# A fused attention and gated feed-forward kernel: each engine's instructions given as a fixed sequence from the kernel's own list schedule

## The chip, the cores and the metric

The kernel runs on one core of one Trainium2 chip. The metric is the device time of one execution in microseconds; lower is better. Before the change three runs gave 1300.32, 1300.39 and 1302.6 us, median 1300.39.

## The reference

Attention with queries pooled in pairs, then a gated feed-forward block whose gate mixes along the sequence. Batch 8, 8 heads, 1152 keys, 576 pooled queries, head size 64; model width 512, inner width 1024.

```python
q_pool = q.reshape(B, H, S // 2, 2, D).mean(axis=3)
scores = matmul(q_pool, k.transpose(0, 1, 3, 2)) / sqrt(D)
attn = exp(scores - scores.max(-1)); attn = attn / (attn.sum(-1) + 1e-09)
x = matmul(attn, v).transpose(0, 2, 1, 3).reshape(B, S // 2, H * D)
h = maximum(x @ w_in, 0); u, g = h[..., :512], h[..., 512:]
g_n = (g - g.mean(-1)) / sqrt(g.var(-1) + 1e-06)
g_s = einsum('ts,bsd->btd', w_spatial, g_n) + b_spatial[None, :, None]
out = (u * g_s) @ w_out
```

## The kernel before

Work is staged by *head pairs*, two heads of one batch: 32 of them, numbered i. Every matrix is split into a large and a small half-precision part, so a product of two matrices is two or three matmuls.

For a head pair `prep` scales queries and keys, splits them, and lays the parts out by DMA in `qhi`, `khi`, `klo`, `xq` and `qd` (ACT L138, L141, L311, L313; DVE L144; POOL L298, L314; a dozen DMAs, L305 to L323). `maxima` makes the scores once coarsely, 27 matmuls of 384 columns (L341, L350), each reduced on DVE (L356). The maxima are then transposed on PE (L371) and enter the precise scores as two more rows. `attention` makes these in 18 steps of 512 queries (L524, L525) and some tail pieces; ACT takes the exponential (L530, L538), and POOL subtracts the rounded part from what it was rounded from (`split`, L542, on 128x1024). `values` multiplies by the values (L444, L448, L453: twelve matmuls of 64 or 65 columns a step), four steps or more later. `turn_main` transposes the result (L475) and writes it as `xg` (ACT L417, DVE L418).

The two weights arrive as doubles. `from_double` decodes a piece of 128x512 in five DVE instructions (L155, L158, L160, L164, L166) and two on ACT; there are twelve pieces. A *unit* is the feed-forward block of two batches: `gated_unit` runs after the eight head pairs that feed it (L601, L665, L706, L749 on PE; the norm L637, L643 on DVE), in the background of the next eight. The last of the four units runs after all attention.

The program is traced by Python generators which are advanced in turn: maxima of i+1, values ahead, prep of i+2, weights and the unit are each moved a little at every step of the attention of i. What is traced is not the final order. The framework's scheduler orders the instructions of each engine by its own estimates, and each engine then runs its list strictly from the front: the first instruction that is not ready holds all behind it. SP issues all DMAs from one such list.

PSUM tiles come from pools: `ps_s` three (pss), `ps_m` two (pm), `ps_w` two (pw), `ps_o` one (o). A third pm tile can be written only when the last reader of the first one is done. So a *slot* joins PE to DVE and ACT: PE stands until a reduction, or the copy of `xg`, has emptied it.

Of the kernel before, what the change touches and what calls it, by code (L numbers as in the profile page):

```python
# [10 lines left out]
F16 = mybir.dt.float16  # L11
BF16 = mybir.dt.bfloat16
F32 = mybir.dt.float32
I32 = mybir.dt.int32
I64 = mybir.dt.int64
U32 = mybir.dt.uint32
# [3 lines left out]
PSUM = bass.MemoryType.PSUM  # L20
# [8 lines left out]
PEXP = 2.0 ** 6  # L29


@with_exitstack
def attn_sgu_kernel(ctx: ExitStack, tc: tile.TileContext, qT, kT, v, w_in, w_spT, b_sp, w_out, out):
    nc = tc.nc
    P = 128
    B, NHP, _, D, _, S = qT.shape
# [18 lines left out]
    D1 = D + 1  # L55
    VW = 2 * D + 2

    const = ctx.enter_context(tc.tile_pool(name="const", bufs=1))
    ld = ctx.enter_context(tc.tile_pool(name="ld", bufs=1))
    pp = ctx.enter_context(tc.tile_pool(name="pp", bufs=4))  # L60
    pt_ = ctx.enter_context(tc.tile_pool(name="pt_", bufs=1))
    wk = ctx.enter_context(tc.tile_pool(name="wk", bufs=2))
    mo = ctx.enter_context(tc.tile_pool(name="mo", bufs=1))
    sm = ctx.enter_context(tc.tile_pool(name="sm", bufs=1))
    ps_s = ctx.enter_context(tc.tile_pool(name="ps_s", bufs=3, space=PSUM))
    ps_m = ctx.enter_context(tc.tile_pool(name="ps_m", bufs=2, space=PSUM))
    ps_o = ctx.enter_context(tc.tile_pool(name="ps_o", bufs=1, space=PSUM))
    ps_w = ctx.enter_context(tc.tile_pool(name="ps_w", bufs=2, space=PSUM))


    nc.scalar.preload_act_table_set("natural_log_exp_and_others")
# [203 lines left out]
    def values_ahead(i):  # L275
        if i + NHP < NP:
            yield from norm_v(i + NHP)
        if i + 1 < NP:
            yield from split_v(i + 1)
# [47 lines left out]
    def maxima(i):  # L327
        st = state[i]
        qhl, khh, X = st["qhl"], st["khh"], st["X"]
        W = KEYS // 3  # L330
        NB = W // P
        mt = sm.tile([P, NT, 3], F32, name="mt", bufs=2)
        for t in range(NT):
            for n in range(3):

                if units or (t + n) % 2:
                    pm = ps_m.tile([P, 512], F32, name="pm")
                else:
                    pm = ps_w.tile([P, 512], F32, name="pw")
                if t == 4:  # L340
                    nc.tensor.matmul(  # L341
                        pm[:, :W],
                        lhsT=qd[i % 2].rearrange("p h s -> p (h s)"),
                        rhs=st["kn"][:, n * NB : (n + 1) * NB, :],
                        start=True, stop=True,
                    )
                else:
                    h = 0 if t < 4 else 1
                    c0 = t * P if t < 4 else TAIL + (t - 5) * P
                    nc.tensor.matmul(  # L350
                        pm[:, :W],
                        lhsT=qhl[:, h, c0 : c0 + P],
                        rhs=khh[:, h, n * NB : (n + 1) * NB, :],
                        start=True, stop=True,
                    )
                nc.vector.reduce_max(out=mt[:, t, n : n + 1], in_=pm[:, :W], axis=AX.X)  # L356
                yield

            if t == 4 and True:
                yield from shift(X, mt, 0, 5)  # L360
        yield
        yield from shift(X, mt, 5 if True else 0, NT)
# [40 lines left out]
    xs = {}  # L403
# [392 lines left out]
    def step(gen):  # L796
        return None if gen is None or next(gen, StopIteration) is StopIteration else gen
# [13 lines left out]
    def drain(gen):  # L811
        while gen is not None:
            gen = step(gen)
# [13 lines left out]
    for i in range(NP):  # L827
        if i + 2 < NP:
            load_kq(i + 2)
        run = [  # L830
            Pace(maxima(i + 1), MAX_RATE) if i + 1 < NP else None,
            Pace(values_ahead(i), V_RATE),
            Pace(prep(i + 2), PREP_RATE, PREP_AT) if i + 2 < NP else None,
            Pace(weights, W_RATE, W_AT if i == 0 else 0),
        ]
# [17 lines left out]
        turn(last=True)  # L853
    for g in units:
        drain(g)


def _lay(inputs):
# [42 lines left out]
```

## Time and profile before

| what | us |
|---|---|
| median of three runs | 1300.39 |
| the profiled execution, whole | 1304.26 |
| its span, first to last instruction | 1302.1 |
| PE busy, of the span | 1179.4 |
| ACT busy | 978.1 |
| DVE busy | 903.9 |
| POOL busy | 847.8 |

PE is TensorE's matmuls, DVE VectorE, ACT ScalarE, POOL GpSimd, SP the engine that issues DMAs. Three stages can be told apart by what runs in them. The first exponentials are at 38.9 us, and attention then runs without a unit until the first matmul of a unit at 302.8. From there on three units run beside attention until the last of the attention's work is near, about 1171. What remains is mostly the fourth unit. The whole execution is 2.2 us longer than its span.

### The profile page before, as it was taken

Reading aid. Unit: us, or ns where it says so; the run is one execution under the profiler, and the core shown is the slowest. Engines: PE = TensorE matmul, PEld = TensorE weight load, DVE = VectorE, ACT = ScalarE, POOL = GpSimd, SP = SyncE. Lnnn points to the kernel's source line nnn. Section 1 sums busy time; section 2 is a strip of 40 time slices with the busy share of each in tenths; the row PEclk is TensorE's granted clock in tenths of the full one; section 3 lists DMA queues with packets and bytes.
Section 4 is the critical chain, followed back from the end, with each engine's and each line's share of the span. In section 5 each row is a group of like instructions: output and inputs, shape, how many; then the busy total and the mean of one; then the engine's idle time right before and its main releaser. Section 6 shows DMA issues by size and latency. Waiting matters only on the chain.

```text
span 1302.1 us, 33821 instructions
## 1 busy us (share of the span) xinstructions
PE 1179.4 (91%) x13632; PEld 734.2 (56%) x13632; DVE 903.9 (69%) x2096; ACT 978.1 (75%) x1689; POOL 847.8 (65%) x494
## 2 busy tenths in 40 slices
PE   3888787789999999899998999899997999999998
PEld 1455554555555666566664666566654666555454
DVE  4689989986778567865669576865669756751545
ACT  5888888889977887878767877878775886755333
POOL 3798897888755766767675767767765666664000
PEclk9989999999999999999999999999998999999999
DMA  7555353435422333154233332155333211101002
GB/s 251 168 166 153 109 162 104 124 95 161 116 87 84 107 107 107 39 144 151 83 100 91 98 115 76 38 149 148 90 107 88 66 52 45 32 34 42 1 1 73
DMA packets 64029, 129.04 MB, mean 99 GB/s; under 512 B 13888, under 2 KB 22080, under 8 KB 63872
## 3 DMA queue, kind: packets, MB, share of 16 engines
q1 hardware_dynamic: 63872, 126.88, 33.7%
q8 instruction: 107, 1.75, 0.6%
q14 instruction: 50, 0.41, 0.1%
HBM read 83.56 MB, written 9.44 MB: 71 GB/s over the span
## 4 chain that ended last, share of the span: by engine, by line
PE 57%; DVE 21%; ACT 9%; POOL 6%; issue 4%; DMA 3%; POOLq 0%; SPq 0%; ACTq 0%; DVEq 0%
DVE mt L356 7%; PE pm L350 6%; PE pss L525 6%; PE pss L524 6%; PE pw L706 6%; PE pw L601 5%; PE pw L749 4%; POOL pt L542 4%; PE pw L665 3%; PE o L453 3%; PE o L444 3%; ACT pt L530 3%; PE o L448 3%; DVE vv L144 2%; DVE row L637 2%
## 5 line engine op out<-in xcount | busy, mean ns | idle before, releaser
L542 POOL TENSOR_TENSOR pt<-pt 128x1024 f16<-128x1024 f32 x288 | 565.6, 1969 | 226.6 <-ACT pt L530 221.4
L530 ACT ACTIVATE pt<-pss,lnp,esc 128x512 f32<-128x512 f32 x576 | 441.8, 779 | 145.5 <-PE pss L525 134.9
L356 DVE TENSOR_REDUCE mt<-pm 128x1 f32<-128x384 f32 x730 | 392.2, 552 | 142.0 <-PE pm L350 125.8
L525 PE MATMUL pss<-xq,klo 66*128 66x64 f16 (+1 forms) x1152 | 279.1, 292 | 0.0
L524 PE MATMUL pss<-qhi,khi 128*128 128x64 f16 (+1 forms) x1152 | 273.5, 291 | 3.2 <-ACT ptl L538 1.7
L350 PE MATMUL pm<-khi,qhi 128*128 128x384 f16 x652 | 213.0, 331 | 26.1 <-DVE mt L356 22.1
L444 PE MATMUL o<-vp,pt 128*128 128x65 f16 x2304 | 229.9, 195 | 6.2 <-DVE xm L461 6.1
L448 PE MATMUL o<-vp,pt 128*128 128x64 f16 x2304 | 228.8, 194 | 0.0
L444 PEld LDWEIGHTS <-pt 128*128 128x128 bf16 x2304 | 183.3, 99 | 71.8 <-DVE xm L461 11.0
L448 PEld LDWEIGHTS <-pt 128*128 128x128 bf16 x2304 | 169.2, 99 | 59.2 <-issue 15.8
L453 PE MATMUL o<-vp,pt 128*128 128x65 f16 x2304 | 170.2, 195 | 19.5 <-POOL pt L542 18.8
L453 PEld LDWEIGHTS <-pt 128*128 128x128 f16 x2304 | 113.0, 99 | 29.8 <-POOL pt L542 25.6
L525 PEld LDWEIGHTS <-klo 66*128 66x128 f16 x1152 | 98.2, 99 | 39.9 <-issue 11.2
L524 PEld LDWEIGHTS <-khi 128*128 128x128 f16 x1152 | 102.4, 100 | 28.4 <-issue 12.9
L272 POOL TENSOR_TENSOR vp<-vt,vp 128x576 f16<-128x576 f32 x64 | 82.6, 1291 | 45.1 <-ACT vp L270 45.0
L350 PEld LDWEIGHTS <-qhi 128*128 128x128 f16 x768 | 75.8, 100 | 63.2 <-issue 12.9
L542 POOL TENSOR_TENSOR ptl<-ptl 128x1152 f16<-128x1152 f32 x32 | 70.4, 2199 | 56.5 <-ACT ptl L538 56.4
L314 POOL TENSOR_TENSOR klo<-kt,kn 128x640 f16<-128x640 f32 x64 | 88.3, 1385 | 11.5 <-ACT kn L313 11.3
L538 ACT ACTIVATE ptl<-pss,lnp,esc 128x256 f32<-128x256 f32 (+1 forms) x128 | 75.5, 590 | 18.2 <-PE pss L525 18.1
L601 PE MATMUL pw<-wi_h,xg 128*128 128x512 f16 x240 | 89.1, 378 | 0.0
L356 DVE TENSOR_REDUCE mt<-pw 128x1 f32<-128x384 f32 x134 | 71.5, 544 | 17.0 <-PE pw L350 16.1
L665 PE MATMUL pw<-xg,wi_h 128*128 128x512 f16 (+1 forms) x336 | 82.0, 331 | 0.0
(180 smaller groups left out, 2356.8 us busy)
## 6 DMA issues: line engine op xcount, KB each, us to landing
vt<-in_v_dram SPq DMA_DIRECT2D x64, 576.0 KB
qt<-in_qT_dram SPq DMA_DIRECT2D x32, 576.0 KB
kt<-in_kT_dram SPq DMA_DIRECT2D x32, 576.0 KB
khi<-kn SPq DMA_DIRECT2D x128, 144.0 KB
out_dram<-row SPq DMA_DIRECT2D x24, 256.0 KB
qhi<-xq SPq DMA_DIRECT2D x64, 72.0 KB
klo<-klo SPq DMA_DIRECT2D x32, 144.0 KB
vv<-in_w_in_dram SPq DMA_DIRECT2D x8, 512.0 KB
```

The lines of the kernel that those rows point to most:

```text
L314: nc.gpsimd.tensor_sub(KL[:, 0, a:z], k0[:, a:z], kn[:, a:z])
L350: nc.tensor.matmul(pm[:, :W], lhsT=qhl[:, h, c0 : c0 + P], rhs=khh[:, h, n * NB : (n + 1) * NB, :], start=True, stop=True,)
L356: nc.vector.reduce_max(out=mt[:, t, n : n + 1], in_=pm[:, :W], axis=AX.X)
L444: nc.tensor.matmul(o[:, t], lhsT=top[:, cols], rhs=vp[:, D : D + D1], start=c == 0 and t == 0, stop=False, skip_group_check=True,)
L448: nc.tensor.matmul(o[:, t, 0:D], lhsT=top[:, cols], rhs=vp[:, 0:D], start=False, stop=False, skip_group_check=True)
L453: nc.tensor.matmul(o[:, t], lhsT=rst[:, cols], rhs=vp[:, D : D + D1], start=False, stop=c == NC - 1, skip_group_check=True,)
L524: nc.tensor.matmul(o, lhsT=khh[:, h, c, :], rhs=qhl[:, h, q], start=True, stop=False)
L525: nc.tensor.matmul(o, lhsT=KL[0:KR, h, c, :], rhs=X[0:KR, h, q], start=False, stop=True)
L530: nc.scalar.activation(pt, ps, AF.Exp, bias=lnp, scale=esc)
L542: nc.gpsimd.tensor_sub(t.bitcast(F16)[:, :, 0::2], t, t.bitcast(BF16)[:, :, 1::2])
L601: nc.tensor.matmul(ph, lhsT=xa[:, cc, c0 : c0 + P], rhs=wa[:, cc, DH:DF], start=n == 0, stop=n == 3 * NCC - 1,)
L665: nc.tensor.matmul(pu[:, : z - a], lhsT=wa[:, cc, fc * P : (fc + 1) * P], rhs=xa[:, cc, a:z], start=n == 0, stop=n == 3 * NCC - 1,)
```

## The change

The traced program is the same, instruction for instruction. New is a class `Order`. Its `pool` wraps every tile pool so that each tile's name, number and number of buffers are known. At the end of the kernel `pin` takes the traced instructions, finds which must wait for which (`edges`), gives each a duration from a small table (`cost`) and makes a list schedule: again and again it takes the engine whose next instruction can start soonest, and on it the earliest traced one that is ready by then. On DVE and POOL, instructions whose inputs all lie in SBUF exclude each other in the table's time. The order that comes out is handed to the framework as a chain of dependencies on each engine.

```diff
+    def edges(self, prog):
...
+                    used = users.setdefault(name, [])
+                    used.append(n)
+                    pre.add(used[0])
...
+    def cost(self, lane, ins):
...
+        if lane == "PE":
+            n = count(xs[0])
+            t = max(28.5, n / 2.4 + 2.5)
+            if xs[0].dtype == F32:
+                t = 110 if n == 128 else max(224, 4 * n / 2.4)
+            return t, t + 148
+        if lane == "SP":
+            big = max((count(x) * x.ap[0][1] * self.SIZE[x.dtype] for x in xs), default=0)
+            return 500, 2400 + big / 230
+        n = max((count(x) for x in xs), default=1)
+        psum = any(self.slot.get(x.tensor.name, (0, 0))[1] for x in xs)
+        if lane == "Activation":
+            t = 1.04 * n + (230 if psum else 95)
+        elif lane == "DVE":
+            t = 1.04 * n + 130
+        else:
+            t = (1.75 if any(x.dtype in (F16, BF16) for x in xs[:-1]) else 2.2) * n + 120
+        return t - 80, t
...
+    def pin(self, tc):
...
+        before = self.edges(prog)
...
+        for _ in prog:
+            best = None
+            for e, ns in ready.items():
+                if ns:
+                    t = max(free[e], min(due[n] for n in ns))
+                    n = min(n for n in ns if due[n] <= t)
+                    if best is None or t < best[0]:
+                        best = (t, e, n)
+            t, e, n = best
+            ready[e].remove(n)
+            own, out = cost[n]
+            if shared[n]:
+
+                if e == "DVE":
+                    if t >= held[0]:
+                        t = max(t, held[1] - 130)
+                    dve = t + out
+                else:
+                    t = max(t, dve)
+                    held = (t, t + out)
+            if e == "SP":
+                wire = max(wire, t + own) + (out - 2400)
+                end = wire + 1900
+            else:
+                end = t + out
+            free[e] = t + own
+            if e in last:
+                tc.add_manual_dep(prog[n], last[e], dep, reason="order")
+            last[e] = prog[n].name
...
-    const = ctx.enter_context(tc.tile_pool(name="const", bufs=1))
+    order = Order()
+    const = order.pool(ctx.enter_context(tc.tile_pool(name="const", bufs=1)), 1)
...
     for g in units:
         drain(g)
+    order.pin(tc)
```

What moved is read from the order of the built programs. The kernel's lines stand 195 lower in the changed file, so L316 is L511 there; a number behind a tile's name tells the tiles of one name apart.

**The start of the program.** The first maxima (L350) need both halves of `khi0`, two DMAs from `kn_163`. On SP, before, they stand four rows apart (L316, L317), ahead of the next bulk loads:

```order
L316 DMA khi0_116<-kn_163 64x1152
L305 DMA qhi0_119<-xq0_113 64x576
L306 DMA qhi0_119<-qhi0_119 64x576
L308 DMA qd0_122<-xq0_113 64x64 x2
L317 DMA khi0_116<-kn_163 64x1152
L318 DMA qhi0_119<-xq0_113 64x576
```

On SP now, from the first of the two (L511) to the second (L512):

```order
L511 DMA khi0_116<-kn_163 64x1152
L517 DMA klo0_107<-klo0_107 64x1152
L426 DMA kt_178<-in_kT_dram 128x1152
L425 DMA qt_346<-in_qT_dram 128x1152
L379 DMA vv_420<-in_w_in_dram 128x512
L432 DMA vt_186<-in_v_dram 128x2x576
L503 DMA qd0_122<-xq0_113 64x64
L513 DMA qhi0_119<-xq0_113 64x576
L512 DMA khi0_116<-kn_163 64x1152
```

Four bulk loads have moved in between: keys, queries, a piece of the weights and values. (`edges` lets every later user of a tile wait for the tile's first one; L512 is traced second on `khi0`, so in the schedule it waits for L511 to land.)

On DVE at the same place, before, one piece of the weights is decoded around the first reductions (`mt_203`):

```order
L155 TENSOR_SCALAR vv_420<-vv_420 128x512
L158 SCALAR_TENSOR_TENSOR u_419<-vv_420,u_419 128x512
L160 TENSOR_SCALAR vv_420<-vv_420 128x512
L164 SCALAR_TENSOR_TENSOR vv_420<-vv_420 128x512
L356 TENSOR_REDUCE mt_203<-pw_204 128x1
L356 TENSOR_REDUCE mt_203<-pw_210 128x1
L166 TENSOR_TENSOR u_419<-u_419,vv_420 128x512
```

On DVE now; two whole pieces stand ahead of the first row shown:

```order
L350 TENSOR_SCALAR vv_420<-vv_420 128x512
L353 SCALAR_TENSOR_TENSOR u_419<-vv_420,u_419 128x512
L355 TENSOR_SCALAR vv_420<-vv_420 128x512
L551 TENSOR_REDUCE mt_203<-pw_204 128x1
L551 TENSOR_REDUCE mt_203<-pw_210 128x1
L551 TENSOR_REDUCE mt_203<-pw_216 128x1
L359 SCALAR_TENSOR_TENSOR vv_420<-vv_420 128x512
L551 TENSOR_REDUCE mt_203<-pw_222 128x1
L551 TENSOR_REDUCE mt_203<-pw_228 128x1
L361 TENSOR_TENSOR u_419<-u_419,vv_420 128x512
```

Decoding has moved forward: at the last of these 27 reductions four pieces and three of the five instructions of a fifth stand ahead on DVE, where it was one piece and one instruction. Ten of these instructions stand between the first and the last of the reductions now, eight of them ahead of the first maxima's transpose (L367 and L371); before it was two, one of them ahead of it.

**A turn of a head pair beside a unit.** The result of head pair 17 is transposed into a pm tile (`pm_11723`), and the next maxima (`pm_11730`, L341) need that slot. On PE, before:

```order
L665 MATMUL pw_11783<-xg_5739,wi_l_127 128x512
L444 LDWEIGHTS pt_11616
L444 MATMUL o_11787<-vp0_101,pt_11616 128x65
L448 LDWEIGHTS pt_11616
L448 MATMUL o_11787<-vp0_101,pt_11616 128x64
L444 LDWEIGHTS pt_11616
L444 MATMUL o_11787<-vp0_101,pt_11616 128x65
L341 LDWEIGHTS qd1_123
L341 MATMUL pm_11730<-kn_11209,qd1_123 128x384
```

On PE now:

```order
L720 MATMUL pss_11973<-xq0_113,klo0_107 128x512
L860 LDWEIGHTS wi_h_126
L860 MATMUL pw_11918<-xg_5739,wi_h_126 128x512
L860 LDWEIGHTS wi_l_127
L860 MATMUL pw_11918<-xg_5739,wi_l_127 128x512
L536 LDWEIGHTS qd1_123
L536 MATMUL pm_11730<-kn_11209,qd1_123 128x384
```

The maxima stand later: more `values` steps and score products have moved ahead of them. On DVE, before, the two norms L637 stand together ahead of what frees the slots, L122 and L418:

```order
L356 TENSOR_REDUCE mt_11519<-pm_11717 128x1
L633 TENSOR_TENSOR rs_11589<-rs_11589,pm_11588 128x9
L637 TENSOR_SCALAR row_11708<-vv_10428,mv_10430,rs_11589 128x512
L637 TENSOR_SCALAR row_11748<-vv_10428,mv_10430,rs_11589 128x512
L122 TENSOR_SCALAR pm_11721<-pm_11721 128x2
L127 TENSOR_SCALAR qkr_11777<-pm_11721 128x2
L643 TENSOR_TENSOR vv_10428<-row_11708,vv_10428 128x512
L418 TENSOR_TENSOR xg_11064<-pm_11723,xg_11064 128x512
```

On DVE now; the first norm (`row_11708`) stands nine rows ahead of the second:

```order
L838 TENSOR_TENSOR vv_10428<-row_11708,vv_10428 128x512
L551 TENSOR_REDUCE mt_11519<-pm_11701 128x1
L551 TENSOR_REDUCE mt_11519<-pm_11717 128x1
L832 TENSOR_SCALAR row_11748<-vv_10428,mv_10430,rs_11589 128x512
L317 TENSOR_SCALAR pm_11721<-pm_11721 128x2
L328 TENSOR_REDUCE vt_12447<-vsq_10268 128x1
L613 TENSOR_TENSOR xg_11064<-pm_11723,xg_11064 128x512
```

One norm, not two, is left between the reductions and the instructions that free the slots.

More of the change, by code (lines that the diff above doesn't have):

```diff
@@ L56, in attn_sgu_kernel @@
     VW = 2 * D + 2
-    const = ctx.enter_context(tc.tile_pool(name="const", bufs=1))
[L59 to L68, printed above, removed]
+    order = Order()
+    const = order.pool(ctx.enter_context(tc.tile_pool(name="const", bufs=1)), 1)
+    ld = order.pool(ctx.enter_context(tc.tile_pool(name="ld", bufs=1)), 1)
+    pp = order.pool(ctx.enter_context(tc.tile_pool(name="pp", bufs=4)), 4)
+    pt_ = order.pool(ctx.enter_context(tc.tile_pool(name="pt_", bufs=1)), 1)
+    wk = order.pool(ctx.enter_context(tc.tile_pool(name="wk", bufs=2)), 2)
+    mo = order.pool(ctx.enter_context(tc.tile_pool(name="mo", bufs=1)), 1)
+    sm = order.pool(ctx.enter_context(tc.tile_pool(name="sm", bufs=1)), 1)
+    ps_s = order.pool(ctx.enter_context(tc.tile_pool(name="ps_s", bufs=3, space=PSUM)), 3, True)
+    ps_m = order.pool(ctx.enter_context(tc.tile_pool(name="ps_m", bufs=2, space=PSUM)), 2, True)
+    ps_o = order.pool(ctx.enter_context(tc.tile_pool(name="ps_o", bufs=1, space=PSUM)), 1, True)
+    ps_w = order.pool(ctx.enter_context(tc.tile_pool(name="ps_w", bufs=2, space=PSUM)), 2, True)
     nc.scalar.preload_act_table_set("natural_log_exp_and_others")
```

118 lines of the change are left out of this document (added).

## Prediction, made before the result was seen

> **What bounds the kernel now.** I read the page first, then the stages, then what PE waits for in the longest one.
>
> ```profile
> span 1302.1 us, 33821 instructions
> 0.00:40.00 40.00, 15.56 (x40) 4.88 (x41) 21.98 (x52) 23.80 (x48) 13.82 (x21) 1.00 0.74 243
> 40.00:303.00 263.00, 212.68 (x2862) 143.45 (x2862) 228.85 (x483) 228.34 (x393) 226.51 (x124) 0.96 0.48 138
> 303.00:1171.00 868.00, 824.67 (x9797) 520.20 (x9795) 599.11 (x1435) 674.42 (x1158) 590.57 (x342) 0.99 0.32 91
> 1171.00:1302.00 131.00, 126.46 (x938) 65.69 (x936) 53.96 (x130) 51.55 (x93) 16.86 (x9) 1.00 0.09 29
> ```
>
> After the length of a stretch the columns are busy PE, PEld, DVE, ACT, POOL, then the granted clock, DMA share and GB/s. Four stages follow. The start (0 to 40) is latency. In attention alone (40 to 303) DVE, ACT and POOL are each busy 226 to 229 of 263 us, and PE less. Beside the units (303 to 1171) PE is busy 95% and no other engine over 78%: there every us that PE stands idle, 868 - 824.7 = 43.3, is a us of the kernel. At the end (1171 to 1302) PE is idle 4.5. The amount of work is the same after the change; only idle time can go or come.
>
> What PE waits for in the third stage, in total, times, longest:
>
> ```profile
> PE pm L341 <- DVE xg L418: 17.1, 8, 2.9
> PE pm L350 <- DVE mt L356: 9.2, 13, 1.4
> PE o L453 <- POOL pt L542: 3.0, 7, 0.8
> PE pw L707 <- ACT u L675: 2.9, 3, 1.5
> PE pm L350 <- DVE xt L502: 2.6, 3, 1.2
> PE pm L371 <- DVE mx L367: 1.9, 4, 0.7
> PE pm L496 <- DVE mt L356: 1.4, 1, 1.4
> PE pw L706 <- DVE u L716: 1.2, 6, 0.2
> ```
>
> These are 39.3 of the 43.3 us, and nearly all are slots: PE stands at a maxima matmul whose pm tile DVE has not emptied, while `values` that are ready stand behind it. The largest, at the turn of head pair 17:
>
> ```profile
> 681.76 4.12 DVE L637 TENSOR_SCALAR row<-vv,mv,rs 128x512 f32<-128x512 f32 x2
> 686.66 0.68 DVE L418 TENSOR_TENSOR xg<-pm,xg 128x512 f16<-128x512 f32 x1
> 688.40 0.54 DVE L637 TENSOR_SCALAR row<-vv,mv,rs 128x512 f32<-128x512 f32 x1
> 687.40 0.32 PE L341 MATMUL pm<-kn,qd 128*128 128x384 f16 x1 [2.92 <-DVE xg L418]
> ```
>
> Two norms took 4.12 us, 2.06 each, where a third took 0.54: POOL's split was running. So DVE came late to the slot, and PE stood 2.92 us.
>
> **The third stage, term by term.** I compare the *cushion* of each such place in the two orders: the PE work that stands between the last matmul on the old tile of the slot and the matmul that waits for it. Its unit prices are start-to-start times:
>
> ```profile
> 802.96 0.38 PE L524 MATMUL pss<-qhi,khi 128*128 128x512 f16 x1
> 803.18 0.38 PE L525 MATMUL pss<-xq,klo 66*128 66x512 f16 x1
> 803.40 0.19 PE L444 MATMUL o<-vp,pt 128*128 128x65 f16 x1
> 803.43 0.19 PE L448 MATMUL o<-vp,pt 128*128 128x64 f16 x1
> 174.44 0.47 PE pm L475 x4
> ```
>
> So 0.22 us for 512 columns, 0.03 for 64, some 0.11 for a float32 transpose; by columns, 0.16 for 384. At head pair 17 the cushion before was one sum and four transposes (0.55), 27 `values` matmuls (0.82) and five of 512 columns (1.08), 2.46 us in all. In the new order it is 4.91. The gain of 2.45 covers all but 0.5 of the 2.92. The other places, worked out alike along PE's rows in both orders, waits in brackets:
>
> - L341 for `xg`: 2.46 to 4.91 at three places (2.92 each), 3.48 to 6.90 at two (2.64), 1.88 to 3.24 (1.62), 1.71 to 3.38 (1.23), 2.15 to 2.09 (0.24). What is not covered is about 2.0; 15 of 17.1 go.
> - L350 for `mt`: most of the 13 grow by over 0.9 (1.56 to 2.50, 1.08 to 2.88, 1.65 to 2.50 three times); one stays at 1.78. 1.6 is left; 7.6 go.
> - L707: 1.24 to 3.65 at all three, 2.9 go. L350 for `xt` (1.90 to 2.75), L371 and L496: 2.6 + 1.9 + 1.3 go. A few single waits: 0.9.
> - L706: 2.18 to 1.96 at six places, 1.3 lost.
> - L453 for POOL has no pool slot; 3.0 stays as it is.
>
> Sum: 15 + 7.6 + 2.9 + 2.6 + 1.9 + 1.3 + 0.9 - 1.3 = 31 us of old waits go.
>
> Against it stand places where nothing waits now and the cushion shrinks. I took all 1422 slot reuses of this stage and held the cushion against the time that the old tile took, in this trace, from its last matmul to its last reader. At 36 places it was long enough and is too short in the new order, by 26 us together. The same measure makes the order of before short by 122 us where PE really stood 43, since one late reduction is counted at each slot behind it and PE's standing is itself in the times. I scale by that ratio, 0.35: 9 us of new waits. The bounds are 0 and 26.
>
> The clock follows the waits:
>
> ```profile
> 303.00:400.00 97.00, 89.50 (x1002) 0.98 0.37 106
> 990.00:1024.00 34.00, 29.46 (x317) 0.90 0.27 67
> ```
>
> 0.02 of 97 and 0.10 of 34 are 5 us at half speed's loss in two stretches with many waits (2.92, 1.35, 1.43 and 1.19 us in the second). If most of these waits go I expect 3 back; bounds 0 and 5. **Third stage: -31 + 9 - 3 = -25 us**, between -48 (all idle time and all clock) and 0.
>
> **The start.** What set the first maxima, and what will:
>
> ```profile
> 16.94 0.59 SPq L317 DMA_DIRECT2D khi<-kn  x1
> 19.46 0.80 PE L350 MATMUL pw<-khi,qhi 128*128 128x384 f16 x2 [11.52 <-DMA khi<-kn]
> 20.78 0.59 SPq L231 DMA_DIRECT2D kt<-in_kT_dram  x1
> 24.84 1.16 ACT L138 ACTIVATE klo<-kt 128x1152 f16<-128x1152 f32 x1 [1.80 <-DMA kt<-in_kT_dram]
> vt<-in_v_dram SPq DMA_DIRECT2D x64, 576.0 KB
> vv<-in_w_in_dram SPq DMA_DIRECT2D x8, 512.0 KB
> ```
>
> PE starts 2.5 us after the second half of `khi0` is issued. In the new order that half stands behind four bulk loads, 3 x 576 + 512 = 2240 KB. At the 243 GB/s of this stage they take 9.2 us (a single 576 KB load took 24.84 - 20.78 = 4.1). They can be issued from about 15.5, when the first half and `klo0` are out, so I put the first maxima at about 26 instead of 19.5: **+6**, bounds +2 and +9. Behind that eight decoding instructions, not one, stand ahead of the first transpose of maxima:
>
> ```profile
> 35.66 0.68 DVE L155 TENSOR_SCALAR vv<-vv 128x512 int32<-128x512 int32 x1
> 38.97 0.68 DVE L158 SCALAR_TENSOR_TENSOR u<-vv,u 128x512 f32<-128x512 uint32 x1
> ```
>
> 7 x 0.6 to 0.7 is **+4**. Attention begins at about 49, ten later than at 38.9.
>
> **Attention alone.** What was decoded early is missing here: three pieces of five instructions.
>
> ```profile
> L166 DVE TENSOR_TENSOR u<-u,vv 128x512 f32<-128x512 f32 x12 | 16.6, 1384 | 0.0
> L164 DVE SCALAR_TENSOR_TENSOR vv<-vv 128x512 int32<-128x512 int32 x12 | 16.1, 1342 | 1.2 <-ACT vv L162 1.1
> L158 DVE SCALAR_TENSOR_TENSOR u<-vv,u 128x512 f32<-128x512 uint32 x12 | 14.3, 1190 | 1.8 <-ACT u L156 1.8
> L155 DVE TENSOR_SCALAR vv<-vv 128x512 int32<-128x512 int32 x12 | 13.2, 1096 | 0.5 <-DMA vv<-in_w_in_dram 0.5
> L160 DVE TENSOR_SCALAR vv<-vv 128x512 int32<-128x512 int32 x12 | 12.6, 1047 | 0.0
> L542 POOL TENSOR_TENSOR pt<-pt 128x1024 f16<-128x1024 f32 x288 | 565.6, 1969 | 226.6 <-ACT pt L530 221.4
> ```
>
> Five means add to 6.1 us a piece, against some 3 us where POOL rests (0.68 above): DVE waits for POOL inside these durations. Three pieces are 9 us by the bare price and 18 with the waiting. If DVE and POOL together bound this stage the whole comes back, if ACT does, little. I take 10, near the bare price: **-10, and with the start's +10 the two stages come to 0**, bounds -8 and +8. In the last stage the order is almost the same: 0.
>
> The Trainium skill (SBUF — State Buffer, Who interferes with whom) says that the pair of ports shared by VectorE and GpSimd is an exclusive lock, and that issue order decides who blocks. The 2.06 and 0.54 us above agree. By that rule a sequence for each engine does not settle which of two engines comes first.
>
> **The sum.** 1302.1 - 25 + 0 = 1277 us of span, 1279 with the 2.2 us around it. The profiled execution (1304.26) is 3.9 over the median, so the same 25 us give **1300.4 - 25 = 1275 us**.
>
> **The rivals.**
>
> *More goes.* The table's times are good enough that idle time in the third stage nearly vanishes (-43 - 5), and the first two stages win 8: 1300 - 56 = 1244. For it: cushions grow far past the waits at most places. Against: 36 tighter places. The Trainium skill (Perfetto Trace Analysis, Identifying the Most-Contended Engine) calls busy matmul time a bad measure of headroom; LDWEIGHTS is busy 520 of 868 us here, and short waits inside a matmul's 0.19 us do not show as idle, so a little more than 43 might go.
>
> *The waits only move.* What is pulled forward as cushion is missing at the next slot, and the 31 us come back: 1300. For it: PE's work between two head pairs is fixed. Against: the waits named sum to 5% of the stage, and units stand by as filler.
>
> *DVE still comes late.* In the third stage the lock goes against DVE in the new order as well, and the eight turns keep their 17.1: 1275 + 15 = 1290.
>
> *Slower: the table is too short for POOL.* It gives 1.912 us for the split, 1.128 for L272 and 1.240 for L314 by its formula. Here are the rows beside the 1969 ns above:
>
> ```profile
> L314 POOL TENSOR_TENSOR klo<-kt,kn 128x640 f16<-128x640 f32 x64 | 88.3, 1385 | 11.5 <-ACT kn L313 11.3
> L272 POOL TENSOR_TENSOR vp<-vt,vp 128x576 f16<-128x576 f32 x64 | 82.6, 1291 | 45.1 <-ACT vp L270 45.0
> ```
>
> Nine splits, two and two a head pair make 0.51 + 0.33 + 0.29 = 1.1 us. The list puts `values` on PE at the moment the table says a split is done, so if each lag reaches PE at L453, 32 pairs cost 36 us: 1275 + 36 = 1311. It decides once 25 of the 36 show, or with the start's +10 not repaid, 15. Against: `values` run four steps behind, and L453 waits only 3.0 us now with POOL busy 590.57 of 868.
>
> **How the numbers follow.** The forecast (1262 to 1288) gets 0.48, more 0.17, DVE late 0.10, moved waits 0.10, slower 0.15. About 0.2% is what a measurement can tell from no change. Faster by more: 0.48 + 0.17 + 0.10 and a little of the moved ones, 0.76; same 0.08; slower 0.16. The range takes in more and moved, and stops within the slower case: 1246 to 1306.
>
> **What would show it.** PE's wait at L341 for `xg` under 3 us, at L350 for `mt` under 3, and PE idle under 25 in the third stage. The first L350 near 26 us and the first exponential near 49. The first unit's first matmul within 8 us of 302.8. I am wrong if L453's wait for POOL grows past 15 us, if new waits for DVE in the third stage pass 26, or if the first unit starts later than 311.

## The result, and the profile after

The changed kernel took **1248.68 us** (median of four runs, 1246.98 to 1249.81); the kernel before took 1301.49 in the same rounds. The ratio is 0.9581, 95% interval [0.9541, 0.9621]. The forecast was 1275 with a range of 1246 to 1306: the direction and the range held, but the gain is 52.8 us, more than twice the 25 forecast. The profiled execution of the changed kernel took 1249.81 us:

```profile
span 1248.0 us, 33766 instructions
```

Both traces are cut at three marks that can be found in each: the first exponential, the first matmul of the first unit and the first matmul of the last unit. Columns as in the prediction: the stretch, its length, busy PE, PEld, DVE, ACT and POOL, granted clock, DMA share, GB/s. Before, the two stages between the marks:

```profile
38.90:302.80 263.90, 213.16 (x2863) 143.56 (x2862) 229.75 (x485) 229.21 (x394) 226.31 (x124) 0.96 0.49 139
302.80:1200.40 897.60, 853.34 (x10149) 538.61 (x10147) 603.61 (x1448) 690.00 (x1181) 607.62 (x350) 0.99 0.32 90
```

After, all four:

```profile
0.00:49.50 49.50, 15.12 (x47) 5.34 (x48) 32.30 (x67) 28.73 (x58) 14.45 (x21) 1.00 0.73 234
49.50:294.50 245.00, 212.30 (x2838) 140.71 (x2837) 207.28 (x464) 224.80 (x390) 225.28 (x123) 0.96 0.48 135
294.50:1145.90 851.40, 839.33 (x10164) 534.36 (x10163) 595.95 (x1449) 687.89 (x1175) 612.48 (x351) 1.00 0.34 96
1145.90:1248.00 102.10, 97.76 (x587) 47.37 (x585) 50.10 (x118) 36.43 (x70) 0.00 (x0) 1.00 0.08 27
```

The start is 10.6 us longer, attention alone 18.9 shorter, the stretch beside the units 46.2 shorter, the end 0.4 longer. Beside the units PE's idle time fell from 897.60 - 853.34 = 44.3 to 851.40 - 839.33 = 12.1, so 32.2 us of the 46.2 are idle time. The other 14.0 went out of PE's *busy* time, although the matmuls are the same.

What PE still waits for in that stretch (total, times, longest; all rows of the view; lines of the changed file, 195 higher than before):

```profile
PE pw L901 <- DVE u L911: 2.5, 6, 0.4
PE pss L719 <- ACT pt L725: 2.5, 3, 1.2
PE pm L545 <- DVE rs L828: 2.0, 3, 0.7
PE o L648 <- POOL pt L737: 0.8, 2, 0.4
PE pm L536 <- DVE xg L613: 0.7, 2, 0.4
PE o L639 <- DVE xm L656: 0.7, 1, 0.7
PE pw L860 <- ACT u L870: 0.7, 3, 0.2
PE pm L545 <- DVE xt L697: 0.4, 1, 0.4
```

The 17.1 us for `xg` are 0.7, and the 9.2 for `mt` are gone from the list. At the turn of head pair 17, where PE stood 2.92 us, the timeline of the changed kernel (start, duration) now reads:

```profile
660.71 1.18 DVE L832 TENSOR_SCALAR row<-vv,mv,rs 128x512 f32<-128x512 f32 x1
662.26 0.69 DVE L613 TENSOR_TENSOR xg<-pm,xg 128x512 f16<-128x512 f32 x1 [0.24 <-ACT xg L612]
665.70 0.49 PE L536 MATMUL pm<-kn,qd 128*128 128x384 f16 x2
```

`xg` leaves the slot at 662.95, PE comes for it at 665.70, and no bracket stands behind PE's row. The norm still runs into GpSimd (1.18 us here, 0.54 where it does not). Over the whole kernel the two norm lines cost DVE the same, before (first two rows, from the view of groups) and after (last two):

```profile
L637 DVE TENSOR_SCALAR row<-vv,mv,rs 128x512 f32<-128x512 f32 x36 | 35.2, 996 | 0.3
L643 DVE TENSOR_TENSOR vv<-row,vv 128x512 f16<-128x512 f32 x36 | 31.2, 880 | 5.7 <-ACT vv L642 5.7
```

```profile
L832 DVE TENSOR_SCALAR row<-vv,mv,rs 128x512 f32<-128x512 f32 x36 | 31.4, 880 | 0.1
L838 DVE TENSOR_TENSOR vv<-row,vv 128x512 f16<-128x512 f32 x36 | 35.5, 991 | 3.0 <-ACT vv L837 2.9
```

66.4 us before, 66.9 after: in the norms DVE is shut out by GpSimd as long as it was. What changed is what stands around them: at this turn one norm, not two, runs between the transposes and `xg`, and PE comes later. (The five lines of the decoding, which moved forward, fell from 72.8 to 59.2 us, which is most of what DVE's busy time lost, 903.9 to 885.6.)

### The profile page after: what moved, and what is told of

Same layout as the page of the kernel before. It is cut to its first block, busy times and chain, and to the rows that moved or that the text cites. A ratio compares the mean times of both kernels' runs of the same rounds, so it can differ in the third digit from the quotient of the medians.

```text
span 1248.0 us, 33766 instructions
## 1 busy us (share of the span) xinstructions
PE 1164.5 (93%) x13632; PEld 727.8 (58%) x13632; DVE 885.6 (71%) x2096; ACT 977.9 (78%) x1689; POOL 852.2 (68%) x494
## 5 line engine op out<-in xcount | busy, mean ns | idle before, releaser
L551 DVE TENSOR_REDUCE mt<-pm 128x1 f32<-128x384 f32 x730 | 385.7, 550 | 115.3 <-PE pm L545 91.4
L720 PE MATMUL pss<-xq,klo 66*128 66x64 f16 (+1 forms) x1152 | 276.1, 290 | 0.1
L639 PE MATMUL o<-vp,pt 128*128 128x65 f16 x2304 | 224.5, 194 | 1.2 <-DVE xm L656 0.7
L643 PE MATMUL o<-vp,pt 128*128 128x64 f16 x2304 | 223.6, 193 | 0.0
L545 PE MATMUL pm<-khi,qhi 128*128 128x384 f16 x652 | 207.2, 331 | 12.0 <-DVE mt L551 4.6
L639 PEld LDWEIGHTS <-pt 128*128 128x128 bf16 x2304 | 176.8, 98 | 44.7 <-DVE xm L656 5.7
L643 PEld LDWEIGHTS <-pt 128*128 128x128 bf16 x2304 | 166.1, 98 | 32.0 <-issue 0.3
L648 PE MATMUL o<-vp,pt 128*128 128x65 f16 x2304 | 169.1, 194 | 1.8 <-POOL pt L737 1.8
L648 PEld LDWEIGHTS <-pt 128*128 128x128 f16 x2304 | 116.6, 98 | 21.2 <-POOL pt L737 6.8
L467 POOL TENSOR_TENSOR vp<-vt,vp 128x576 f16<-128x576 f32 x64 | 85.3, 1334 | 46.1 <-ACT vp L465 46.1
L901 PE MATMUL pw<-ws_h,vv 128*128 128x512 f16 x216 | 79.5, 379 | 2.7 <-DVE u L911 2.5
```

The costliest lines, as they stand in the source:

```text
L545: nc.tensor.matmul(pm[:, :W], lhsT=qhl[:, h, c0 : c0 + P], rhs=khh[:, h, n * NB : (n + 1) * NB, :], start=True, stop=True,)
L639: nc.tensor.matmul(o[:, t], lhsT=top[:, cols], rhs=vp[:, D : D + D1], start=c == 0 and t == 0, stop=False, skip_group_check=True,)
L643: nc.tensor.matmul(o[:, t, 0:D], lhsT=top[:, cols], rhs=vp[:, 0:D], start=False, stop=False, skip_group_check=True)
L648: nc.tensor.matmul(o[:, t], lhsT=rst[:, cols], rhs=vp[:, D : D + D1], start=False, stop=c == NC - 1, skip_group_check=True,)
L720: nc.tensor.matmul(o, lhsT=KL[0:KR, h, c, :], rhs=X[0:KR, h, q], start=False, stop=True)
L901: nc.tensor.matmul(pv, lhsT=l, rhs=r[:, 0:MAIN], **fl)
```

## The experiments

Each kernel was timed against the kernel before on the same chip. That had a median of 1304.62 us beside "PE's sequence alone", "all sequences but PE's", "no exclusion in the table" and "no wait for first users"; 1304.73 beside "longer table, exclusion", "mean delays", "first stages alone" and "from head pair 8 on"; 1304.27 beside the other four, and 1301.49 beside the change. So 3 us between the change and another run are not a difference. "First stages" are the start and attention alone together.

| run | us | ratio, 95% interval | first stages | beside the units |
|---|---|---|---|---|
| before | 1301.49 | | 302.8 | 897.6 |
| the change | 1248.68 | 0.9581 [0.9541, 0.9621] | 294.5 | 851.4 |
| PE's sequence alone | 1313.82 | 1.0063 [1.0042, 1.0083] | 309.0 | 900.4 |
| all sequences but PE's | 1310.95 | 1.0044 [1.0026, 1.0062] | 314.6 | 891.5 |
| PE's and DVE's | 1318.56 | 1.0102 [1.0059, 1.0144] | 325.9 | 891.1 |
| no exclusion in the table | 1309.25 | 1.0037 [1.0017, 1.0058] | 309.8 | 891.1 |
| longer table, no exclusion | 1288.61 | 0.988 [0.984, 0.992] | 302.9 | 879.9 |
| longer table, exclusion | 1258.34 | 0.964 [0.9607, 0.9673] | 306.5 | 849.5 |
| mean delays | 1258.20 | 0.9636 [0.96, 0.9673] | 301.0 | 857.1 |
| mean delay, DVE alone | 1264.26 | 0.9695 [0.9656, 0.9734] | 301.3 | 859.5 |
| first stages alone | 1305.05 | 0.9989 [0.9963, 1.0015] | 295.5 | 903.9 |
| from head pair 8 on | 1255.96 | 0.9632 [0.9596, 0.9669] | 299.5 | 851.0 |
| no wait for first users | 1252.81 | 0.9598 [0.9573, 0.9623] | 295.6 | 852.7 |
| decoding held | 1266.00 | 0.9702 [0.9668, 0.9736] | 310.1 | 851.4 |

The two right columns come from one profiled execution each. Beside the units the kernels fall into groups: near 850 to 860, 880, and 891 to 904.

### Is it one engine's sequence?

The sequence is handed over for PE alone, for all engines but PE, and for PE and DVE (one line in each run, in this order).

```diff
-            if e in last:
+            if e in last and e == "PE":
...
+            if e in last and e != "PE":
...
+            if e in last and e in ("PE", "DVE"):
```

> The list schedule is made as in the change, but only PE's sequence is handed to the framework; the other engines keep the framework's own order. Theory A (the gain beside the units comes from where PE's work stands, so that ready matmuls lie ahead of the slot waits): most of it stays, 1249 to 1265 us, and PE idle beside the units stays under 20 us. Rival B (it comes from DVE and ACT emptying the slots earlier): 1285 to 1300 us, with PE's waits for DVE beside the units above 25 us.

> The other side of the last one: the sequences of ACT, DVE, POOL and SP are handed over, and PE keeps the framework's order. Theory A: the stage beside the units falls back to about 890 us, and the whole is 1280 to 1305 us. Rival B: most of the gain stays, 1250 to 1265 us.

> The sequence is handed over for TensorE and VectorE alone; ScalarE, GpSimd and SyncE keep the framework's own order. Theory P (the pair that has to agree is TensorE and VectorE, since the waits beside the units are TensorE's for VectorE's tiles): 1250 to 1272 us, with the stretch beside the units at 848 to 870 us. Rival L (VectorE's sequence holds only with GpSimd's own order beside it, or ScalarE's): 1290 to 1320 us.

All three are a little slower than the kernel before, by 0.6, 0.4 and 1.0%: 1313.82 us, 1310.95 and 1318.56. The first and the second lie outside the ranges of both their theories. What PE waits for beside the units, with PE's sequence alone:

```profile
PE pm L545 <- DVE mt L551: 15.4, 14, 2.4
PE pm L536 <- DVE xg L613: 12.8, 8, 4.2
PE pss L719 <- ACT pt L725: 7.1, 8, 1.0
```

With all but PE's:

```profile
PE pm L545 <- DVE mt L551: 23.0, 31, 1.4
PE pm L566 <- DVE mx L562: 4.2, 8, 0.9
PE pm L536 <- DVE xg L613: 0.8, 2, 0.5
```

With PE's and DVE's:

```profile
PE pm L536 <- DVE xg L613: 9.5, 6, 3.4
PE pss L719 <- ACT pt L725: 8.6, 10, 1.2
PE o L648 <- POOL pt L737: 6.8, 9, 2.1
```

The lists of all engines but PE take the wait for `xg` away (0.8) and leave PE's own order waiting for the maxima (23.0). With PE and DVE both in sequence the waits for the maxima leave the top of the list, but `xg`, the exponentials and their split come late from engines in another order. Beside the units these two runs are still 6 us shorter than the kernel before; what makes them slower as a whole is the first stages, 314.6 and 325.9 against 302.8. So none of the three subsets has the gain that all lists have together (others were not tried); theory P of the third run fell, and rival L's range took the result.

### What in the table makes the sequence good?

The exclusion between DVE and GpSimd is taken out of the schedule. (In the kernel it holds for three kinds of instruction with all inputs in SBUF, `two_from_sbuf`: tensor with tensor, tensor with scalar, and copies.)

```diff
-        shared = [e in ("DVE", "Pool") and self.two_from_sbuf(i) for e, i in zip(lane, prog)]
+        shared = [False] * len(prog)
```

> The change with one thing taken out of the list schedule's table: DVE and POOL instructions from SBUF no longer exclude each other in its time. Theory C (the table is good because it knows that DVE waits for POOL, 2.06 us against 0.54 for a norm): the waits at L341 for the copies of xg come back, 8 to 25 us slower than the change, 1257 to 1274. Rival D (the cushions are large enough without it): within 4 us of 1249.

It took 1309.25: the whole gain is gone, where 8 to 25 us were expected to go, so both theories missed. The stretch beside the units and three of its waits:

```profile
309.80:1200.90 891.10, 845.15 (x10187) 535.77 (x10185) 606.11 (x1451) 695.45 (x1185) 606.63 (x352) 1.00 0.32 91
...
PE pm L545 <- DVE mt L551: 17.7, 20, 1.5
PE pm L566 <- DVE mx L562: 10.9, 8, 1.7
...
PE pm L536 <- DVE xg L613: 2.2, 6, 1.1
```

What came back is not `xg` (2.2), which theory C had named, but the waits for the maxima and their row `mx`. Without the exclusion the table thinks DVE is done sooner than it is, and PE is sent to the maxima's slots too early. With this table a list schedule as such is worth nothing here. That could still be luck, a good draw among sequences; so the durations of DVE, GpSimd and ScalarE were made 5% longer, with the exclusion and without it:

```diff
+        cost = [(t + u / 20, u + u / 20) if e in ("DVE", "Pool", "Activation") else (t, u) for e, (t, u) in zip(lane, cost)]
```

> The changed kernel with every duration of VectorE, GpSimd and ScalarE in the table 5% longer; the exclusion stays in it, the program stays the same and nearly all of the order moves. Theory C (the gain comes of knowing the exclusion, not of this one sequence): 1243 to 1268 us. Rival N (the sequence of the changed kernel is one lucky draw among sequences that lie between 1250 and 1310): over 1275 us.

> The same 5% longer durations of VectorE, GpSimd and ScalarE as in the run with the longer table, but with the exclusion taken out of the schedule. Theory C/H (VectorE's instructions that meet GpSimd come 528 ns later than the table without the exclusion says, which is 124 us in all, and 5% of VectorE's 886 us are only 44 us, spread over the wrong ones): 1285 to 1320 us, with the stretch beside the units at 880 to 905 us. Rival R (any reserve in the table does; the exclusion is only one way to give it): 1250 to 1275 us.

```profile
306.50:1156.00 849.50, 836.54 (x10199) 534.33 (x10198) 601.94 (x1451) 687.71 (x1179) 615.46 (x352) 1.00 0.34 96
```

```profile
302.90:1182.80 879.90, 843.15 (x10186) 535.87 (x10185) 606.78 (x1451) 696.72 (x1185) 610.42 (x352) 1.00 0.32 93
```

With the exclusion (first fence) much of the order moved (in the two traces, 5629 of PE's 13632 positions hold another line of the kernel), and the stretch is 849.5, as good as the change's. The first stages are 12.0 longer; I put such differences between one good sequence and the next down to luck, and no run shows their cause. Without it (second fence) it is 879.9: longer durations are a reserve that helps by 11 us over the bare table beside the units, and by 20.6 on the whole. Theory C held in both by the time (its stretch of 880 to 905 just missed), and rival R has a third of the 60.6 us between no exclusion and the change. The 5% are 44 us of DVE's time, where the exclusion is 124. A larger reserve on all instructions, 124 us spread evenly, was not tried, so it is not shown how much hangs on *which* instructions get it.

Then the exclusion was replaced by its mean: no exclusion, but each instruction that takes part in it is as much longer as it was delayed on the mean in the change's own schedule; then DVE's part alone.

```diff
-        shared = [e in ("DVE", "Pool") and self.two_from_sbuf(i) for e, i in zip(lane, prog)]
+        extra = [{"DVE": 528, "Pool": 145}[e] if e in ("DVE", "Pool") and self.two_from_sbuf(i) else 0 for e, i in zip(lane, prog)]
+        cost = [(t + x, u + x) for (t, u), x in zip(cost, extra)]
+        shared = [False] * len(prog)
```

> The table of durations knows no exclusion between VectorE and GpSimd, but each instruction that takes part in it gets the mean delay that the exclusion had in the changed kernel's own schedule: 528 ns on each of 235 VectorE instructions, 145 ns on each of 480 GpSimd ones. Theory W (the sequence must know when VectorE is shut out): no better than without the exclusion, 1290 to 1315 us, with VectorE's maxima waited for by TensorE as before. Theory H (it is enough to know how much later VectorE is on the whole): most of the gain stays, 1248 to 1270 us. Between 1270 and 1290 both count.

> As the run with the mean delays, but with VectorE's alone: 528 ns on each of its 235 instructions that take part in the exclusion, and no delay on GpSimd's. Theory D (VectorE's lateness is the whole of it): 1250 to 1268 us, as with both delays. Rival G (GpSimd's 145 ns on each of 480 instructions, 70 us in all, set when TensorE can have the exponentials): 1275 to 1310 us, with TensorE waiting for the split of the exponentials for more than 10 us beside the units.

I had thought that the sequence must know *when* DVE is shut out (theory W). With both means it took 1258.2, inside theory H's range, with 857.1 us beside the units and the wait at L547 for the maxima at 1.8:

```profile
301.00:1158.10 857.10, 843.06 (x10149) 532.42 (x10148) 616.09 (x1447) 689.09 (x1182) 613.85 (x351) 1.00 0.33 94
...
PE o L650 <- POOL pt L739: 3.1, 7, 1.0
...
PE pm L547 <- DVE mt L553: 1.8, 4, 0.8
```

Without GpSimd's 145 ns it took 1264.3, inside theory D's range, and the wait for the split of the exponentials went from 3.1 to 5.6:

```profile
PE o L650 <- POOL pt L739: 5.6, 10, 1.7
```

So most of what the exclusion brings comes with a mean lateness of the DVE instructions that take part in it. From no exclusion to the change it is 1309.25 - 1248.68 = 60.6 us; the two means bring 51.1 of them, DVE's alone 45.0. The other 9.5 can't be put down to knowing the moment, since the longer table with the exclusion lost as much; beside the units the mean costs 5.7 (857.1 against 851.4).

The Trainium skill (SBUF — State Buffer, Who interferes with whom) calls the pair of ports an exclusive lock whose loser blocks fully. The trace agrees: two norms of 2.06 us each beside GpSimd splits of 2.1, 0.54 where GpSimd rests. From it I had argued that fixed sequences do not settle who comes first. The meetings did stay (66.4 and 66.9 us of norms), and the gain came all the same: the schedule has to reckon with DVE's lateness, it need not prevent it.

### Do the stages add?

The sequence is handed over only for what is traced before head pair 8, and only for what is traced from it on:

```diff
+        if i == 2 * NHP:
+            order.mark = len(tc.nc.cur_bb.bb.instructions)
...
+        early = {i.name for i in list(tc.nc.cur_bb.bb.instructions)[: self.mark]}
...
+            if e in last and prog[n].name in early and last[e] in early:
...
+            if e in last and prog[n].name not in early and last[e] not in early:
```

> The sequence is handed over only for instructions traced before head pair 8 (the start and the attention that runs alone); the rest is left to the framework's own order. If the stages add as the two traces show (start +10.6, attention alone -18.9): about 8 us under the kernel before, 1288 to 1298 us, with the stretch beside the units at 891 to 900 us. Rival: the hand-over from one order to the other costs a turn of waits, and the gain of the first stages is given back: 1300 to 1310 us.

> The sequence is handed over only for instructions traced from head pair 8 on; the first stages are left to the framework's own order. If the stages add: 46 us off the kernel before, 1252 to 1266 us, with the first exponential near 39 to 41 us, the attention alone at 260 to 268 us and the stretch beside the units at 848 to 856 us. Rival: the sequence counts on the state in which its own first stages leave the engines, and the waits beside the units come back in part: 1270 to 1300 us.

The late part alone took 1255.96, as the sum of the stages says, with its own stretch as in the change:

```profile
299.50:1150.50 851.00, 839.18 (x10164) 534.28 (x10163) 593.91 (x1450) 687.61 (x1179) 613.55 (x351) 1.00 0.33 95
```

The early part alone won its 7.3 us (295.5 against 302.8) and no time on the whole, 1305.05; its stretch beside the units was 903.9 in the profiled execution:

```profile
295.50:1199.40 903.90, 857.20 (x10148) 540.70 (x10147) 607.17 (x1449) 687.53 (x1172) 609.18 (x351) 0.99 0.31 89
```

The rival's time came, but its mechanism, a turn of waits at the hand-over, shows little. Of the 6.3 us that this stretch is longer than before, idle time is 2.4 (46.7 against 44.3) and PE's busy time 3.9. The executions differ with the granted clock: three of the ten took 1295.97 to 1299.3 us at 0.991 to 0.992, the other seven 1303.64 to 1307.51 at 0.981 to 0.987. Of the kernel before, the five executions at 0.991 to 0.992 took 1299.0 to 1300.2, so at an equal clock two of the three are 3 to 4 us faster, a part of the 7.3.

### The start, and the decoding

Two places of the first stages that the prediction priced. In the first run the later users of `khi`, `qhi`, `klo`, `xq` and `qd` no longer wait, in the schedule, for the tile's first user, so the second half of `khi0` need not wait for the first half to land.

```diff
-                    pre.add(used[0])
+                    if not (k0 := a[0][0]).startswith(("khi", "qhi", "klo", "xq", "qd")):
+                        pre.add(used[0])
```

> The change with the rule left out, for the tiles khi, qhi, klo, xq and qd alone, that a tile's later users wait for its first one; the two halves of the first khi then stand together on SP, ahead of four bulk loads. If those loads were the price of the start, the first maxima come at about 19 to 21 us instead of 28.1, and the first exponential at about 43 to 46 instead of 49.5, since DVE still decodes in between. Theory E (the start's delay is paid in full, since attention alone is bound by engines that are busy all the time): the whole is 4 to 8 us faster, 1241 to 1245. Rival F (the decoding done while DVE waits for khi would have to be done later anyway): within 2 us of 1249.

In the second, the decoding of every piece of the weights but the very first is held in the schedule until the first exponential (in `pin`, `first` is that instruction).

```diff
+        first = next(n for n, i in enumerate(prog) if names[i.engine] == "Activation" and "pt" in writes(i))
+        for h in self.hold:
+            n = next(at[i.name] for i in every[h:] if i.name in at and names[i.engine] == "DVE")
+            before[n].add(first)
...
+            first = name == "wi"
...
+                if j or not first:
+                    order.hold.append(len(tc.nc.cur_bb.bb.instructions))
```

> In the schedule, the decoding of the weight pieces from the second one on is held until the first exponential. Theory E (the decoding that the sequence puts ahead of the first exponential is why the attention alone got 19 us shorter while the start got 11 us longer): first exponential at 39 to 45 us, attention alone 254 to 264 us instead of 245, the first unit no earlier than now (294 to 304 us), the whole 1246 to 1262 us. Rival S (the attention alone is shorter because of the order of the maxima and rows, and the decoding is only in the way of the start): first exponential at 39 to 45 us, attention alone 243 to 250 us, the first unit at 283 to 292 us, the whole 1237 to 1246 us.

The first one's maxima started at 17.9 instead of 28.1 (the view of one line: duration least/median/most, first and last start), yet its first exponential came at 46.5, only 3.0 earlier, and its attention alone took 249.1, 4.1 longer:

```profile
L546 PE MATMUL pw<-khi,qhi x116: 322/326/527, 17.9 to 870.6; 128*128 128x384 f16 x116
```

```profile
0.00:46.50 46.50, 14.58 (x36) 4.31 (x37) 31.50 (x65) 27.74 (x55) 14.74 (x21) 1.00 0.72 238
46.50:295.60 249.10, 211.55 (x2846) 140.64 (x2845) 210.80 (x466) 225.56 (x392) 217.78 (x122) 0.95 0.49 137
```

The whole, 1252.81, lies outside both theories' ranges (1241 to 1245, and 1247 to 1251), and by the intervals it cannot be told from the change.

The second one's first exponential came at 47.5, not at 39 to 45, so both theories missed there. Its attention alone took 262.6:

```profile
47.50:310.10 262.60, 216.70 (x2843) 143.61 (x2842) 223.12 (x476) 230.84 (x404) 221.43 (x122) 0.94 0.47 134
```

The 17.6 us against the change's 245.0 are theory E's: what attention alone won was the early decoding. (The whole, 1266.0, is 4 over E's range: the start gave back only 2.0, and the first unit came at 310.1, not by 304.) The last of the five instructions of a piece, in that stage with decoding held (first fence) and in the change (second):

```profile
L369 DVE TENSOR_TENSOR u<-u,vv 128x512 f32<-128x512 f32 x11 | 14.2, 1290 | 0.0
```

```profile
L361 DVE TENSOR_TENSOR u<-u,vv 128x512 f32<-128x512 f32 x8 | 10.8, 1345 | 0.0
```

Three pieces more are decoded there by these rows (four by some of a piece's other instructions): 17.6 us, 4.4 to 5.9 a piece.

No run was faster than the change. The two edits of this section were not tried together.

## Why the prediction was wrong in size, step by step

The step that failed is "only idle time can go or come". The sum for the stretch beside the units held PE's idle time and 3 us of clock; the runs showed 14.0 us gone from PE's busy time as well. Two more terms were too small: the decoding taken out of attention alone, and the old waits, whose count left out that DVE would free the slots sooner. Term by term:

- **The start, +10 forecast, +10.6 measured.** The first maxima stood at 28.05 (forecast about 26), the first exponential at 49.5 (about 49). The split into +6 for the late load and +4 for the decoding is not confirmed: taking either away gave back 3.0 and 2.0 of the 10.6. So the sum came true without its parts being shown, which is partly luck; what the rest of the 10.6 is stays open.

```profile
28.05 0.80 PE L545 MATMUL pw<-khi,qhi 128*128 128x384 f16 x2 [19.80 <-DMA khi<-kn]
```

- **Attention alone, -10 forecast, -18.9 measured.** The mechanism, early decoding, was right; the term was mis-sized by the choice between two prices. I took 3 us a piece, the bare price. The price with the waiting for GpSimd, 6.1 a piece and 18 for three, stood beside it, and holding the decoding back cost 4.4 to 5.9. I had written that the whole comes back if DVE and POOL together bound this stage, and I took a value near the other case without giving a reason. This is 9 of the 29 us that the forecast's span lacked.
- **Old waits beside the units, -31 forecast.** Of today's 12.1 us of idle, those of a new kind or grown are 2.5 (exponentials) + 2.0 (`rs`) + 0.7 + 0.7 + 1.3 (L901, which had 1.2) = 7.2. So 4.9 of the old 44.3 are left and 39.4 went. The cushion count left too much: 2.0 for `xg` (measured 0.7), 1.6 for `mt` (none), 3.0 at L453 (0.8 today, for which I had no mechanism), and the idle time that no row of the list named. And its mechanism is only half of it. It set PE's new order against DVE's times of before. With PE's sequence alone, which comes nearest to that, `xg` still cost 12.8 us and `mt` 15.4; the lists of the other engines alone brought `xg` to 0.8. What the count missed is that DVE frees the slot sooner. The transposes of head pair 17, before and after:

```profile
681.98 0.63 PE L475 MATMUL pm<-ident,xm 128*128 128x128 f32 x4
660.97 0.63 PE L670 MATMUL pm<-ident,xm 128*128 128x128 f32 x4
```

  From their start to the end of `xg` it was 5.36 us (to 687.34) and is 1.98 (to 662.95), so at this turn the earlier release alone is more than the wait of 2.92. For `mt` neither side alone took the waits away (15.4 and 23.0). That the sum came within 8 us is partly luck.
- **New waits, +9 forecast, 7.2 measured.** The scaled measure held by size; that these waits stand at the 36 places is not shown.
- **PE's busy time, -3 forecast, -14.0 measured.** This is the largest error, 11 us. I counted only the clock, and said under a rival that short waits inside a matmul's time do not show as idle, without giving them a price. Of the 14.0, the clock can be no more than about 7: the kernel before had three stretches below full clock,

```profile
386.00:396.00 10.00, 8.49 (x73) 0.83 0.24 75
984.00:992.00 8.00, 4.87 (x34) 0.79 0.05 10
998.00:1012.00 14.00, 11.38 (x108) 0.76 0.49 128
```

  and 0.17 x 10 + 0.21 x 8 + 0.24 x 14 = 6.7 us; the change has 1.00 in each of its 100 us slices from 300 to 1100. The rest are short waits. I took each start-to-start time of PE's matmuls in the two traces against the median for its shape, less what shows as idle: at full clock such excess is 25.5 us before and 17.0 now, 8.5 less, and under the slow clock it was 6.0. The run without the exclusion bears that out: with the waits back and full clock in each slice from 300 to 1100, its busy time is 845.15, 5.8 above the change's. The Trainium skill (Perfetto Trace Analysis, Identifying the Most-Contended Engine) warns that matmul busy time is not a good measure of how close a kernel is to its limit. The trace agrees, with 14.0 us of it gone at the same matmuls.
- **The end, 0 forecast, +0.4 measured.**

Together: 11 us of PE's busy time, 9 of decoding and 10 of idle time (32.2 against the 22 net of the forecast) are the difference. What came true is the rival *more goes* (1244 us, chance 0.17): idle time mostly gone, the first two stages 8.3 better against its 8. That its time is within 5 us is in part luck, for it had 43 us of idle time and 5 of clock beside the units, where 32.2 of idle time and 14.0 of busy time went. I held 36 tighter places against it, and the new waits came to about what I had said; I had not asked what in PE's busy time was waiting.

Of the signs, `xg` under 3 (0.7), `mt` under 3, idle under 25 (12.1), the first exponential near 49 held; the first unit's matmul came 8.3 us before 302.8, just outside the 8 named. The rival in which GpSimd's short table makes the kernel slower did not come: L648 waits 0.8 us beside the units, although its split takes 1.97 us against the table's 1.912. Nor did DVE late through the lock: the lock cost the norms as much as before, but the schedule had allowed for it. Nor did the waits only move: 7.2 us of new ones stand against 39.4 that went.

## What to carry to other kernels

A fixed sequence for in-order engines is as good as the lateness it assumes: with durations that left out one shared resource it was no better than the framework's own order, and a mean delay on the instructions that use it brought back 51 of 61 us (5% on all instructions of three engines, 21). Here the engines' lists gained only together: PE's alone, PE's and DVE's, and all but PE's were each slightly worse than none. In a stretch where one engine is busy 95%, price the waits that hide inside its busy time too, and price an engine's moved work by what it costs in that stretch, waiting included, when the engines that share a resource bound it.

## What the hardware showed that was not expected

The granted clock did not follow the sum of the waits, as the prediction had it. The run without the exclusion has as many waits beside the units as the kernel before (891.10 - 845.15 = 46 us of idle time), and full clock through slices in which PE stood 7 us of 100:

```profile
300.00:400.00 100.00, 93.40 (x1107) 1.00 0.40 115
400.00:500.00 100.00, 92.84 (x1133) 1.00 0.36 104
```

The kernel before, in the first of these slices:

```profile
300.00:400.00 100.00, 92.50 (x1042) 0.98 0.39 113
```

What differs is the longest single wait, 2.9 us before and 1.7 without the exclusion. In the kernel before, at the wait of 2.92 us that ends at 387.5, and behind it:

```profile
384.00:388.00 4.00, 1.08 (x17) 1.00 0.02 6
388.00:392.00 4.00, 4.00 (x27) 0.61 0.50 166
```

Beside the units, the five traces whose longest wait is 2.8 to 4.2 us have two to five such falls of the clock each; the nine whose longest wait is 1.7 us or less have one fall between them. Not every long wait is followed by one (the 2.92 us at head pair 17 are not), and no run changed a wait's length alone, so the cause is not shown.

The clock is a small part of the gain. At a granted clock of 0.991 to 0.992 five executions of the kernel before took 1299.0 to 1300.2 us; the change took 1246.98 to 1249.81 at 0.992 to 0.993, still about 50 less.
